# A hand-placed attention and SwiGLU kernel: the order of its last 621 statements is replaced by another one

## The chip, the cores and the metric

The kernel runs on one core of a Trainium2 chip. The metric is the device time of one execution in microseconds (us). Three runs of the kernel before gave 215.81, 215.92 and 216.0, so the median is 215.92. One more execution was recorded by the profiler; all durations here come from that one.

A core has five engines with an instruction queue each: TensorE (PE in the profile, with its weight loads listed as PEld), VectorE (DVE), ScalarE (ACT), GpSimd (POOL) and SyncE (SP), which only issues transfers. Each engine takes its instructions in the order in which the program gives them and waits at an instruction until its operands are there and its output may be written.

## The reference

Block-wise linear attention with a decay per head, over four batches of 768 tokens, eight heads of 64, feeds a SwiGLU feed-forward layer:

```python
for b in range(nb):                       # blocks of 64 tokens
    intra = np.einsum('bhic,bhjc->bhij', qb, kb) * Dmask[None]
    intra = np.einsum('bhij,bhjd->bhid', intra, vb)
    inter = np.einsum('bhid,bhde->bhie', qb * lam_pow[None], kv_state)
    out[:, :, sl] = intra + inter
    kv_state = lam_block * kv_state + np.einsum('bhsd,bhse->bhde', kb * rev_pow[None], vb)
x = out.transpose(0, 2, 1, 3).reshape(3072, 512)
g = x @ w_gate                            # 512 x 1536
return (g / (1 + np.exp(-g)) * (x @ w_val)) @ w_out      # 1536 x 512
```

## The kernel before, in words

**Groups and tiles.** The tokens are cut into twelve groups `g`. A group is one pair of 128-token blocks of one batch. Two groups make a tile `t` of 512 tokens, so there are six tiles, 0 to 5.

**Attention of a group.** `load_fp32` (L103) brings k, q and v from memory by SP. `kcast` (L277) and `qcast` (L281) cast, `v_scale` (L257) multiplies v by its decay (line L260), and `dma_transpose` (L265) has SP transpose q and k. The rest is on TensorE, in 64x64 tiles. `scores` multiplies q and k (L347 for groups up to 5, L383 for the later ones); `mask` (L356) multiplies the scores by the causal decay on DVE. `upd_mm` (L390, matmuls in L408) forms a group's part of the state, which `sadd`, `kvn`, `kvm` and `kv0c` accumulate on DVE, ACT and POOL. `inter` (L530, L541) applies the state to q, and `intra` (L547, L554) adds the masked scores times v to the same PSUM banks. Between the two stands `guard` (L523), an ACT copy of one column out of one of these banks (L525), so that `intra` starts only once `inter` is done. `evr` (L566) casts the sum into the tile's x.

**Feed-forward of a tile.** Tiles 0 to 3 use `ffn_gate` (L592, matmuls L600, SiLU on ACT L605) and `ffn_val` (L607, matmuls L618, product on DVE L622), one call for each 128 columns of d_ff. Tiles 4 and 5 use `uprod` (L731, L755) in the blocks that `unit` opens, a form with seven products in place of eight, whose combined operands come from `w_combo` and `x_combo`; `silu` and `mu` finish them. The output product of tile 0 is `ffn_out` (L629, L638). That of tiles 1 to 5 is `oprod` (L799, L814): `oprod(t, g, k)` is product k of group g, again seven of them, with sums of columns from `hsum`. After some k, ACT or DVE copies a quarter of the result into an output buffer (L817 to L829).

**Stores.** `store(t, g, r, c0, c1)` (L792, transfer L795) writes columns c0 to c1 of one 128-token block: 256 KB for 512 columns. SP issues it. The last product of the kernel, `oprod(5, 1, 3)`, brings its own stores: half of the result is copied by ACT and stored by ACT's queue, the other half copied by DVE and stored by SP, 64 KB each:

```python
        if k == 3 and last and g:
            for c, (fn, eng) in enumerate(((act, nc.scalar), (dve, nc.sync))):
                c0, c1 = c * HD // 2, (c + 1) * HD // 2
                fn(out=O[0][:, HD + c0:HD + c1], in_=Bb[:, c0:c1])
                store(t, g, 0, HD + c0, HD + c1, eng)
```

**The order.** From the end of the helper functions on, the kernel is a flat list of calls. The order of the list is the order on every engine: no scheduler moves anything (`tc.manual_schedule()`). A call that issues work on several engines puts it at this place in each of their queues. `use(6); ffn_gate(1, 8, 0, 2)` says into which of the eight PSUM banks the next call writes; `unit` and `out_new` name six banks for a group of products. A call that takes a bank waits until the bank's last reader, on ACT or DVE, has finished. The attention matmuls of a group are placed among the feed-forward matmuls of earlier tiles, so that masks and casts have time to run beside full matmuls. In the part that the change touches (L1035 to the end), the 64x64 matmuls come in 18 unbroken stretches, which this text calls visits.

Of the kernel before, what the change touches and what calls it, by code (L numbers as in the profile page):

```python
# [37 lines left out]
def _body(ctx, tc, nc, q, k, v, lam, moe_w_gate, moe_w_val, moe_w_out, out):  # L38
# [998 lines left out]
    mask(3, 1, 0)  # L1037
    mask(3, 0, 0)
    mask(3, 0, 1)
# [3 lines left out]
    use(7); ffn_val(1, 8, 0, 2)  # L1043
    mask(3, 1, 1)
    use(2); ffn_gate(1, 9, 0, 2)
    use(4); ffn_gate(1, 10, 0, 2)
    use(6); ffn_val(1, 9, 0, 2)
    use(0, 1); op_new(3)
    inter(3, True)
    use(2); ffn_val(1, 10, 0, 2)  # L1050
    guard(3)
    intra(3, False)
    use(3, 4); upd_mm(4)
    evr(3, 0, DVEC)
    kcast(5)
    evr(3, 1, ACTC)
    use(7); ffn_gate(1, 11, 0, 2)
    sadd(3, 1)
    sadd(4, 0)
    use(2); ffn_val(1, 11, 0, 2)  # L1060
    kvn(4, 0, ACTC)
    use(6); ffn_gate(1, 0, 2, 4)
    use(1); ffn_gate(1, 1, 2, 4)
    use(0); ffn_gate(1, 2, 2, 4)
    sadd(4, 1)
    qcast(5, nc.vector)
    use(5); ffn_gate(1, 3, 2, 4)
    use(2); ffn_val(1, 1, 2, 4)
    use(7); ffn_val(1, 2, 2, 4)
    use(6); ffn_val(1, 0, 2, 4)  # L1070
    use(1); ffn_gate(1, 4, 2, 4)
# [4 lines left out]
    use(3); ffn_gate(1, 5, 2, 4)  # L1076
    use(2, 0, 6, 4); scores(4)
    v_scale(5, nc.gpsimd)
    kvm(3, nc.gpsimd)
    wo_cast()  # L1080
    wo_cast()
    wo_cast()
    wo_cast()
    mask(4, 0, 1)
    mask(4, 1, 1)
    use(3); ffn_val(1, 3, 2, 4)
    mask(4, 1, 0)
    use(5); ffn_gate(1, 6, 2, 4)
    use(7); ffn_val(1, 4, 2, 4)
    use(4); ffn_gate(1, 7, 2, 4)  # L1090
    use(3); ffn_val(1, 5, 2, 4)
    use(1); ffn_gate(1, 8, 2, 4)
    use(7, 4); op_new(4)
    use(0); ffn_gate(1, 9, 2, 4)
    use(6); ffn_val(1, 9, 2, 4)
    mask(4, 0, 0)
    use(3); ffn_val(1, 6, 2, 4)
    inter(4, True)
    guard(4)
    w_combo(0, 0, (0, 3))  # L1100
    use(6); ffn_val(1, 7, 2, 4)
    intra(4, False)
    use(3, 5); upd_mm(5)
    evr(4, 1, ACTC)
    evr(4, 0, ACTC)
    new_xt(3)
    use(1); ffn_gate(1, 10, 2, 4)
    use(0); ffn_val(1, 8, 2, 4)
    use(4); ffn_gate(1, 11, 2, 4)
    use(7); ffn_gate(2, 0, 0, 2)  # L1110
    use(0); ffn_val(2, 0, 0, 2)
    wo_cast(ACTC)
    use(2); ffn_gate(2, 1, 0, 2)
    wo_combo(0)
    sadd(5, 0)
    use(1); ffn_val(1, 10, 2, 4)
    wo_cast()
    kvn(5, 0, ACTC)
    use(4); ffn_out(0, 0)
    use(0); ffn_val(1, 11, 2, 4)  # L1120
    use(7); ffn_gate(2, 2, 0, 2)
    use(4); ffn_gate(2, 3, 0, 2)
    use(1, 6); op_new(5)
    inter(5, True)
    use(3, 2, 7, 0); scores(5)
    kvm(4, nc.vector)
    mask(5, 1, 0)
    mask(5, 0, 0)
    mask(5, 0, 1)
    w_combo(1, 0, (0, 3))  # L1130
    sadd(5, 1)
    wo_combo(1)
    mask(5, 1, 1)
    guard(5)
    kcast(6)
    use(4); ffn_out(0, 1)
    qcast(6, nc.vector)
# [3 lines left out]
    load_fp32(7, nc.sync, v, "v")  # L1141
    hs_new(1)
    use(7); ffn_out(0, 2)
    intra(5, False)
    evr(5, 0, ACTC)
    evr(5, 1, ACTC)
    hs_new(1)
    use(2); ffn_out(0, 3)
    hsum(1, 0, 0, 6, 0, 1)
    hsum(1, 0, 0, 6, 1, 2)  # L1150
    hsum(1, 1, 0, 6, 1, 2)
    wo_combo(2)
    hsum(1, 2, 0, 6, 0, 1)
    use(7); ffn_gate(2, 0, 2, 4)
    use(5); ffn_val(2, 1, 0, 2)
    use(0); ffn_val(2, 3, 0, 2)
    use(6); ffn_val(2, 2, 0, 2)
    use(4); ffn_val(2, 0, 2, 4)
    hsum(1, 1, 0, 6, 0, 1)
    use(5); ffn_gate(2, 1, 2, 4)  # L1160
    hsum(1, 2, 0, 6, 1, 2)
    wo_combo(3)
    v_scale(6, nc.vector)
    use(7); ffn_gate(2, 2, 2, 4)
    use(2); ffn_gate(2, 3, 2, 4)
    use(3); ffn_val(2, 2, 2, 4)
    hsum(1, 3, 0, 6, 0, 1)
    use(7); ffn_val(2, 1, 2, 4)
    use(0); ffn_gate(2, 4, 0, 4)
    use(5); ffn_val(2, 4, 0, 4)  # L1170
    use(1); ffn_gate(2, 5, 0, 4)
    kcast(7)
    use(3, 4); scores(6)
    use(6, 2); upd_mm(6)
    mask(6, 0, 1)
    use(7); ffn_val(2, 5, 0, 4)
    sadd(6, 0)
    kvm(5, nc.gpsimd)
# [5 lines left out]
    out_new(1, (0,), [0, 1, 7], 0)  # L1184
    oprod(1, 0, 1)
    kvn(6, 0, ACTC)
    w_combo(0, 1, (0, 3))
    use(4); ffn_val(2, 3, 2, 4)
    sadd(6, 1)
    use(5); ffn_gate(2, 6, 0, 4)  # L1190
    oprod(1, 0, 7)
    oprod(1, 0, 2)
    kvn(6, 1, ACTC)
    v_scale(7, nc.vector)
    sadd(6, 2)
    mask(6, 0, 0)
    kv0c(3, ACTC)
    use(4); ffn_gate(2, 7, 0, 4)
    kvn(6, 2, ACTC)
    oprod(1, 0, 6)  # L1200
    sadd(6, 3)
    use(6); ffn_val(2, 6, 0, 4)
    hsum(1, 3, 0, 6, 1, 2)
    oprod(1, 0, 5)
    oprod(1, 0, 4)
    use(0); ffn_val(2, 7, 0, 4)
    oprod(1, 0, 3)
    store(1, 0, 1, 0, 512, None)
    store(1, 0, 0, 0, 512, None)
    use(3, 7); op_new(6)  # L1210
    inter(6, True)
    use(0, 4); upd_mm(7)
    use(2, 6); scores(7)
    kvm(6, nc.vector)
    sadd(7, 0)
    v_scale(8, nc.gpsimd, 0, 4)
    guard(6)
    kvn(7, 0, ACTC)
    mask(7, 0, 0)
    sadd(7, 1)  # L1220
    intra(6, False)
    evr(6, 1, ACTC)
    use(1); ffn_gate(2, 8, 0, 4)
    kvn(7, 1, ACTC)
    kcast(8)
    sadd(7, 2)
# [457 lines left out]
```

## Time and profile before

| what | value |
|---|---|
| median of three runs | 215.92 us (215.81 to 216.0) |
| the profiled execution's own time | 215.75 us |
| its span (first to last recorded event) | 214.0 us |
| TensorE busy | 207.5 us, 97% of the span, 2801 matmuls |
| DVE, ACT, POOL busy | 157.5, 131.8 and 50.9 us |
| granted TensorE clock | 1.00 |
| moved by DMA | 39.77 MB, 186 GB/s in the mean |
| stores by SP of L795, 256 KB each | median 2.7 us from issue to landing |

How to read it. The shares of busy time are means over the span. The slices divide the span into 40 equal parts and give the busy share of each in tenths. The chain that ended last is followed back from the last instruction, at each step to what released it. A row of the timeline gives the start, the busy time from the start of the first to the end of the last instruction in a run of equal ones, the engine, the line, the operation and the number of instructions; because matmuls are pipelined, the busy time of a row reaches past the start of the next row. In square brackets stands the idle time before and what ended it.

### The profile page before, as it was taken

To read this page: it belongs to the slowest core of one execution; us is meant where nothing else is said; L and a number is where in the kernel's file an instruction comes from. 1 tells how busy PE (TensorE), PEld (TensorE's weight loads), DVE (VectorE), ACT (ScalarE), POOL (GpSimd) and SP (SyncE) were. 2 spreads that over 40 slices of the span, in tenths; PEclk is the share of its full clock that TensorE was granted. 3 is DMA by queue.
4 is the path that set the end of the run, shared out by engine and by line. 5 is a ranking of instruction groups with operands and counts; after the bars stand their busy time and mean duration, and the time that the engine had idled before them with its cause. 6 is when DMAs were issued, how large, how long until landed. Compare 5 with 4: busy or idle time off the path is not lost.

```text
span 214.0 us, 6802 instructions
## 1 busy us (share of the span) xinstructions
PE 207.5 (97%) x2801; PEld 153.0 (72%) x2801; DVE 157.5 (74%) x302; ACT 131.8 (62%) x283; POOL 50.9 (24%) x72
## 2 busy tenths in 40 slices
PE   7799999999999999999999999999999999999993
PEld 3466455888886558767654545888888888888883
DVE  1673447679774798889779899999887589982851
ACT  6788576657446443667677385946873677536522
POOL 6585755704472010300101030040200000000200
PEclk9999999999999999999999999999999999999999
DMA  6999999999996697989677869776000500005014
GB/s 187 343 352 373 378 365 324 266 256 222 356 335 132 168 280 188 240 204 261 156 189 163 208 144 248 185 69 228 6 3 3 196 0 3 0 0 199 0 54 147
DMA packets 82177, 39.77 MB, mean 186 GB/s; under 512 B 45410, under 2 KB 77794, under 8 KB 82146
## 3 DMA queue, kind: packets, MB, share of 16 engines
q1 hardware_dynamic: 80946, 38.74, 66.7%
q10 hardware_dynamic: 1200, 0.59, 1.0%
q8 instruction: 22, 0.36, 0.7%
q14 instruction: 9, 0.07, 0.1%
HBM read 28.31 MB, written 6.29 MB: 162 GB/s over the span
## 4 chain that ended last, share of the span: by engine, by line
PE 92%; SPq 3%; DMA 2%; POOL 1%; issue 0%; ACT 0%; DVE 0%
PE bank L814 22%; PE bank L600 20%; PE bank L618 20%; PE bank L755 17%; PE bank L638 5%; SPq L109 2%; DMA v<-in_v_dram 2%; PE bank L541 2%; PE bank L554 2%; PE bank L408 1%; PE bank L347 1%; POOL v_s L260 1%; PE bank L383 1%; PE bank L310 0%; ACT kvf L501 0%
## 5 line engine op out<-in xcount | busy, mean ns | idle before, releaser
L622 DVE TENSOR_TENSOR h<-sil,bank 128x256 bf16<-128x256 bf16 (+1 forms) x67 | 35.0, 532 | 21.4 <-PE bank L618 17.2
L618 PE MATMUL bank<-xt,wv_sb 128*128 128x256 bf16 (+1 forms) x276 | 50.2, 314 | 0.0
L600 PE MATMUL bank<-xt,wg_sb 128*128 128x256 bf16 (+1 forms) x276 | 50.1, 315 | 0.0
L605 ACT ACTIVATE sil<-bank 128x256 bf16<-128x256 f32 (+1 forms) x67 | 31.6, 477 | 22.3 <-PE bank L600 15.7
L618 PEld LDWEIGHTS <-wv_sb 128*128 128x128 bf16 x276 | 26.6, 98 | 14.7
L600 PEld LDWEIGHTS <-wg_sb 128*128 128x128 bf16 x276 | 26.1, 98 | 12.9
L260 POOL TENSOR_TENSOR v_s<-v,dec 128x512 bf16<-128x512 f32 (+1 forms) x15 | 18.6, 1254 | 60.9 <-DMA v<-in_v_dram 19.8
L814 PEld LDWEIGHTS <-h 128*128 128x128 bf16 x240 | 23.5, 98 | 3.6
L814 PE MATMUL bank<-wo_sb,h 128*128 128x256 bf16 x180 | 22.3, 273 | 0.0
L814 PEld LDWEIGHTS <-hs 128*128 128x128 bf16 x180 | 17.5, 98 | 3.4 <-DVE hs L673 0.2
L362 DVE TENSOR_TENSOR ssb<-bank,causal 128x512 bf16<-128x512 f32 x24 | 15.5, 684 | 3.6 <-PE bank L347 3.5
L814 PE MATMUL bank<-wt,hs 128*128 128x256 bf16 x120 | 15.6, 272 | 0.0
L755 PEld LDWEIGHTS <-ws 128*128 128x128 bf16 x144 | 14.0, 98 | 1.8
L755 PE MATMUL bank<-xs,ws 128*128 128x256 bf16 x96 | 13.9, 272 | 0.0
L763 DVE TENSOR_TENSOR bank<-bank,es 128x512 f32<-128x512 f32 x12 | 8.3, 697 | 7.2 <-PE bank L755 4.4
L780 DVE TENSOR_TENSOR h<-sil,bank 128x512 bf16<-128x512 bf16 x18 | 11.8, 679 | 1.5 <-ACT sil L774 1.2
L780 POOL TENSOR_TENSOR h<-sil,es 128x512 bf16<-128x512 bf16 x1 | 1.2, 1162 | 46.7 <-DVE es L765 46.7
L774 ACT ACTIVATE sil<-bank 128x512 bf16<-128x512 f32 x18 | 10.2, 593 | 2.1 <-PE bank L755 2.1
L638 PE MATMUL bank<-wo_sb,h 128*128 128x512 bf16 x48 | 10.9, 379 | 0.0
L755 PE MATMUL bank<-xt,wv_sb 128*128 128x256 bf16 x72 | 10.8, 273 | 0.0
L443 ACT CAST kvn<-kvf 64x256 bf16<-64x256 f32 x22 | 8.9, 403 | 3.1 <-DVE kvf L489 2.7
L278 ACT CAST qk<-kraw 128x1024 bf16<-128x1024 f32 x9 | 9.4, 1042 | 1.8 <-DMA kraw<-in_k_dram 1.8
(127 smaller groups left out, 342.9 us busy)
## 6 DMA issues: line engine op xcount, KB each, us to landing
out_dram<-osb SPq DMA_DIRECT2D x22, 256.0 KB, 2.7
v<-in_v_dram SPq DMA_DIRECT2D x18, 256.0 KB, 4.3
woraw<-in_moe_w_out_dram SPq DMA_DIRECT2D x6, 512.0 KB, 9.1
kraw<-in_k_dram SPq DMA_DIRECT2D x24, 128.0 KB, 3.2
qraw<-in_q_dram SPq DMA_DIRECT2D x24, 128.0 KB, 3.8
wraw<-in_moe_w_gate_dram SPq DMA_DIRECT2D x5, 512.0 KB, 6.9
wraw<-in_moe_w_val_dram SPq DMA_DIRECT2D x5, 512.0 KB, 6.7
kraw<-in_k_dram SPq DMA_DIRECT2D x4, 512.0 KB, 6.3
```

Source lines behind the costliest of these rows:

```text
L260: eng.tensor_tensor(out=st[("vs", g)][:, h0:h1], in0=st[("v", g)][:, h0:h1].rearrange("p h (s d) -> p h s d", s=2), in1=vfac(g, h0, h1), o ...
L278: fn(out=qk_new(g)[:, 0].rearrange("p s (h d) -> p h s d", h=H), in_=st[("kraw", g)].rearrange("p h (s d) -> p h s d", s=2))
L362: nc.vector.tensor_tensor(out=st[("ssb", g)][:, h2, 2 * c:2 * c + 2].rearrange("p a s n -> p a (s n)"), in0=st[("sp", g, c, h2)].rearrange ...
L600: nc.tensor.matmul(gp[:, n0:n1], wg_sb[:, mc, fs], xt[:, g0:g1, mc].rearrange("p g b n -> p g (b n)"), start=(mc == 0 and n0 == 0), stop=( ...
L605: nc.scalar.activation(sil[:, 0:N], gp[:, 0:N], AF.Silu)
L618: nc.tensor.matmul(vp[:, n0:n1], wv_sb[:, mc, fs], xt[:, g0:g1, mc].rearrange("p g b n -> p g (b n)"), start=(mc == 0 and n0 == 0), stop=( ...
L622: nc.vector.tensor_tensor(out=h_sb[:, fc % FH, b0:b1].rearrange("p b n -> p (b n)"), in0=sil[:, 0:N], in1=vp[:, 0:N], op=ALU.mult)
L638: nc.tensor.matmul(ps, st[("h", t, fc // FH)][:, fc % FH, b], wo_sb[:, fc, c0:c1], start=(fc == 0), stop=(fc == FC - 1))
L755: nc.tensor.matmul(o[i][:, fi * 256:fi * 256 + 256], lhs(c, 2 * j + fi), rhs(c), start=(k < 2 and fi == 0 and c == 0), stop=(c == KH - 1), ...
L774: nc.scalar.activation(sil[half, r], unit_src(t, j, half, r)[0], AF.Silu)
L780: eng.tensor_tensor(out=st[("h", t, half)][:, 2 * j:2 * j + 2][:, :, r:B:2], in0=v3(st[("u", t, j)][4][half, r]), in1=v3(unit_src(t, j, ha ...
L814: nc.tensor.matmul(o, lhs(f), rhs(f), start=(k in (1, 7) and f == 0), stop=(f == FH - 1), skip_group_check=True)
```

## The change

The change replaces the list from L1035 to the end by another order of the same 621 statements. No statement is added or dropped. Banks are chosen anew. Two half pieces of `v_scale` and the two `kvm` of groups 3 and 4 trade places between DVE and POOL.

The visits of groups 3, 4, 10 and 11 are joined. A plus sign stands between parts of one visit:

| before | after |
|---|---|
| scores 3 + update 3, inter 3, intra 3 + update 4 | scores 3 + update 3, inter 3 + update 4 + intra 3 |
| scores 4, inter 4, intra 4 + update 5 | scores 4 + inter 4, intra 4 + update 5 |
| scores 11, inter 10 + update 11, intra 10 | scores 11 + inter 10, intra 10 + update 11 |
| the other nine | the same nine, in other surroundings |

That makes 15 visits in place of 18. The stores of tile 1 now stand between `dma_transpose(10)` and the loads of group 11, and one of them between the loads of q and v. Those of tile 4 stand behind the first products of tile 5. Among the last statements, three stores of tile 5 now stand behind `oprod(5, 1, 3)`, which issues stores of its own. The `...` lines mark what is left out of the diff.

```diff
     use(0, 1, 2, 3); scores(3)
     use(4, 5); upd_mm(3)
...
     use(7); ffn_val(1, 8, 0, 2)
+    use(4); ffn_gate(1, 9, 0, 2)
+    sadd(3, 1)
     mask(3, 1, 1)
-    use(2); ffn_gate(1, 9, 0, 2)
-    use(4); ffn_gate(1, 10, 0, 2)
-    use(6); ffn_val(1, 9, 0, 2)
-    use(0, 1); op_new(3)
+    use(2, 4); op_new(3)
+    use(1); ffn_gate(1, 10, 0, 2)
+    use(6); ffn_gate(1, 11, 0, 2)
+    use(7); ffn_val(1, 9, 0, 2)
     inter(3, True)
-    use(2); ffn_val(1, 10, 0, 2)
     guard(3)
+    use(1, 0); upd_mm(4)
     intra(3, False)
-    use(3, 4); upd_mm(4)
     evr(3, 0, DVEC)
...
+    use(2, 5); op_new(4)
+    use(0, 6, 3, 4); scores(4)
+    inter(4, True)
+    v_scale(5, nc.gpsimd)
+    kvm(4, nc.gpsimd)
...
     dma_transpose(10)
+    store(1, 0, 1, 0, 512, None)
+    store(1, 0, 0, 0, 512, None)
     store(1, 1, 1, 0, 512, None)
-    store(1, 1, 0, 0, 512, None)
     load_fp32(11, nc.sync, k, "kraw")
     load_fp32(11, nc.sync, q, "qraw")
+    store(1, 1, 0, 0, 512, None)
     load_fp32(11, nc.sync, v, "v")
...
+    dma_transpose(11)
+    store(2, 0, 1, 0, 512, None)
+    unit(4, 0, (5, 2, 1, 3, 6, 0))
+    uprod(4, 0, 0, 0)
+    uprod(4, 0, 0, 1)
+    oprod(2, 1, 5)
+    uprod(4, 0, 1, 1)
+    uprod(4, 0, 3, 0)
+    silu(4, 0, 0, 0)
+    uprod(4, 0, 1, 0)
+    uprod(4, 0, 2, 0)
+    uprod(4, 0, 2, 1)
+    use(5); ffn_val(3, 5, 0, 4)
+    uprod(4, 0, 3, 1)
...
-    use(5, 3); scores(11)
+    uprod(4, 0, 4, 0)
+    use(5, 7); op_new(10)
+    use(4, 2); scores(11)
+    inter(10, True)
     mask(11, 0, 0)
     mask(11, 0, 1)
-    uprod(4, 0, 3, 0)
-    uprod(4, 0, 2, 1)
-    silu(4, 0, 0, 0)
-    uprod(4, 0, 4, 0)
     uprod(4, 0, 5, 0)
...
+    guard(10)
+    intra(10, False)
+    use(2, 4); upd_mm(11)
...
-    inter(10, True)
-    use(7, 0); upd_mm(11)
...
-    intra(10, False)
...
     store(4, 0, 1, 0, 512, None)
     store(4, 1, 1, 0, 512, None)
+    oprod(5, 0, 2)
     store(4, 0, 0, 0, 512, None)
     store(4, 1, 0, 0, 512, None)
...
-    oprod(5, 0, 1)
-    oprod(5, 1, 1)
-    oprod(5, 0, 2)
+    oprod(5, 1, 7)
+    oprod(5, 1, 6)
+    oprod(5, 0, 7)
+    hsum(5, 3, 4, 6, 0, 2)
+    oprod(5, 0, 6)
+    oprod(5, 1, 5)
+    oprod(5, 1, 4)
+    oprod(5, 0, 5)
+    oprod(5, 1, 2)
     store(5, 0, 0, 0, 256, None)
-    oprod(5, 1, 2)
     store(5, 1, 0, 0, 256, None)
-    oprod(5, 0, 7)
-    oprod(5, 1, 7)
-    oprod(5, 0, 6)
-    oprod(5, 1, 6)
-    hsum(5, 3, 4, 6, 0, 2)
-    oprod(5, 0, 5)
-    oprod(5, 1, 5)
-    hsum(5, 3, 2, 4, 0, 2)
     oprod(5, 0, 4)
+    oprod(5, 0, 3)
+    oprod(5, 1, 3)
     store(5, 0, 1, 0, 512, None)
-    oprod(5, 1, 4)
     store(5, 1, 1, 0, 512, None)
-    oprod(5, 0, 3)
     store(5, 0, 0, 256, 512, None)
-    oprod(5, 1, 3)
```

828 lines of the change are left out of this document (405 added, 423 removed).

## The prediction

> **What bounds the kernel now.** I read the busy shares first (part 1 of the page), then the shares of the chain that ended last (part 4), then the busy time of each engine in single stretches, then single rows of the timeline.
>
> ```profile
> PE 207.5 (97%) x2801; PEld 153.0 (72%) x2801; DVE 157.5 (74%) x302; ACT 131.8 (62%) x283; POOL 50.9 (24%) x72
> ...
> PE 92%; SPq 3%; DMA 2%; POOL 1%; issue 0%; ACT 0%; DVE 0%
> 47.00:210.70 163.70, 163.70 (x2236) 125.17 (x2232) 131.79 (x246) 98.42 (x215) 22.97 (x21) 1.00 0.59 149
> 110.00:130.00 20.00, 20.00 (x212) 9.85 (x210) 17.94 (x30) 13.91 (x30) 3.10 (x3) 1.00 0.75 184
> 130.00:145.00 15.00, 15.00 (x233) 11.89 (x232) 14.13 (x27) 10.38 (x26) 2.53 (x2) 1.00 0.80 153
> ```
>
> TensorE is the bound. The reordered statements start at line 1035, which the trace reaches at about 47 us, and from there to 210.70 PE is busy all 163.70 us (third line of rows: stretch, its length, then busy time and count of PE, PEld, DVE, ACT and POOL, the granted clock, here 1.00, DMA share and GB/s). So in this part only three things can move the time: the matmul work itself with its switches, a wait that PE does not have today, and what comes after the last matmul. The last two lines name the engine that is nearest to causing such a wait: DVE is busy 90% and 94% of these stretches.
>
> **What a visit costs.** The change keeps every matmul and joins stretches of attention matmuls (64x64 tiles), called visits. Counted in the old and new text, from line 1035 on there are 18 before and 15 after. Rows of the timeline (start, busy us, engine, line) around the visit that holds `scores(11)` alone, and one row from inside a longer visit:
>
> ```profile
> 145.28 0.60 PE L755 MATMUL bank<-xt,wv_sb 128*128 128x256 bf16 x4
> 145.81 0.45 PE L383 MATMUL bank<-qkt 64*64 64x64 bf16 x32
> 146.19 0.61 PE L755 MATMUL bank<-xt,wg_sb 128*128 128x256 bf16 x4
> ...
> 147.51 0.60 PE L755 MATMUL bank<-xs,wg_sb 128*128 128x256 bf16 x4
> 147.95 0.60 PE L755 MATMUL bank<-xt,wv_sb 128*128 128x256 bf16 x4
> 121.67 0.44 PE L383 MATMUL bank<-qkt 64*64 64x64 bf16 x32
> 121.93 0.26 PE L408 MATMUL bank<-v_s,qk 64*64 64x64 bf16 x7
> ```
>
> Four full matmuls between full ones go from 147.51 to 147.95, 0.44 us. Those ahead of the visit need 145.28 to 145.81, 0.53: entry 0.09. The 32 small matmuls need 0.26 inside a visit (121.67 to 121.93) and 0.38 when full ones follow (145.81 to 146.19): exit 0.12. A visit therefore costs 0.21 us, and three fewer give 3 x 0.21 = -0.63. Ends: nothing (the price returns inside the joined visits) to -0.9 (the early visits have other matmuls around them, 128x512 and `ffn_out`, and I let them be half as dear again).
>
> The Trainium skill (TensorE: Matmul & The Clock Gate, "Step-by-step: what each phase is for") says that the drain of one matmul overlaps the fill of the next; applied to a switch, that would make a visit free and the sum below 0.63 higher. The row shows 0.09 and 0.12 where it would have none, so here the trace disagrees, and I go by the row; what the rule would make of the time is rival C below.
>
> **The joined visit of group 3.** `guard` is an ACT copy of one column that makes `intra` wait until `inter` has finished in the same banks. Before, four full matmuls stand between them:
>
> ```profile
> 50.02 0.41 PE L541 MATMUL bank<-qkt,kvn 64*64 64x128 bf16 x8
> 50.36 0.61 PE L618 MATMUL bank<-xt,wv_sb 128*128 128x256 bf16 x4
> 50.47 0.16 ACT L525 COPY guard<-bank 128x1 f32<-128x1 f32 x1 [0.34 <-PE bank L541]
> 50.90 0.64 PE L554 MATMUL bank<-ssb,v_s 64*64 64x128 bf16 x32
> ```
>
> The guard ends at 50.47 + 0.16 = 50.63, 0.61 after `inter` starts. After, only `upd_mm(4)` stands between: `inter` 0.34 - 0.12 = 0.22 and 32 update matmuls 0.26, together 0.48. PE waits 0.13, and with the 0.04 that lies between the end of `inter` (50.43) and the guard (50.47) as the way back, 0.17. Ends: 0 (intra's first head free earlier) to 0.5, if ACT is just in a 0.38 SiLU when `inter` ends. Everything behind on PE shifts by this; ACT's and DVE's work shifts with it and gains slack. For groups 4, 10 and 11 full matmuls still separate `inter` from `intra`, so their guards cost nothing.
>
> **The new order of the rest.** Same statements, so the same busy time on each engine; the work of a few `v_scale` and `kvm` pieces only trades places between DVE and POOL. Full matmuls move at no price as long as their banks and operands are there. Walking the new text engine by engine with the rows' durations, the operands arrive 0.1 to 0.9 us ahead of PE. The thinnest: `scores(10)` wants the transposed q and k of `dma_transpose(10)` at about 130.7 and, with the landing of 3.8 us that this transpose has now, gets them at about 130. On SP, the three stores of tile 1 now behind `dma_transpose(10)` (two before) put the loads of group 11 one issue, 0.4 us, later; the last piece of `k` is issued at about 132 and lands 3.0 later, and `kcast(11)`, its first user, runs at 136 today and stands later in the new text; POOL's `v_scale(11)` runs at 139. `store(1,1,0)` between the `q` and `v` loads has its data long since. The output buffers it frees are wanted again by tile 2's copies, some 5 us later. `ffn_val(3,5)` comes late, but its gate's SiLU is done and the columns it feeds are used only by the tile-3 products. Sum of new waits: +0.1. Low end -0.1 (PE has nothing to lose but gaps that the 163.70 does not show), high end +1.5, worked out with the second rival.
>
> **The tail.** Here the text of the change moves work onto the path that ends the span. SP executes its queue in order. Before, `oprod(5,1,3)`, the last product, came after all other stores, and its own 64 KB store by SP was the last thing in the queue:
>
> ```profile
> 211.16 0.29 DVE L833 COPY osb<-bank 128x128 f32<-128x128 f32 x1 [2.16 <-ACT osb L833]
> 211.48 0.33 SPq L795 DMA_DIRECT2D out_dram<-osb  x1
> out_dram<-osb SPq DMA_DIRECT2D x2, 256.0 KB, 2.1
> out_dram<-osb SPq DMA_DIRECT2D x1, 128.0 KB, 1.7
> out_dram<-osb SPq DMA_DIRECT2D x1, 64.0 KB, 1.6
> 166.99 1.82 SPq L795 DMA_DIRECT2D out_dram<-osb  x4
> 168.30:170.30 2.00, 2.00 (x20) 1.80 (x19) 0.37 (x1) 1.78 (x4) 0.00 (x0) 1.00 1.06 407
> ```
>
> The three lines in the middle are the landing times of the tail's stores. After, `store(5,0,1)`, `store(5,1,1)` (256 KB each) and `store(5,0,0)`'s second half (128 KB) stand behind that 64 KB store, which waits for the last DVE copy at 211.45. Before, the last three of these went out between 209.30 and 210.94; now they cannot start before 211.8. Issues back to back: four took 1.82 in the row from 166.99, the first alone 0.33 with a gap, so three more take 1.4. The bytes give the same: 640 KB at the 407 GB/s that four such stores reach (last line) are 655,360 B / 407 GB/s = 1.61. The last store issues at 211.48 + 1.4 = 212.9 and lands 1.7 later, 214.6, where the last landing was 211.48 + 1.6 = 213.1: +1.5. With the bytes a little behind the issues I take +1.6. Ends: +1.1 (three issues of 0.33, landing 0.1 longer) and +2.5 (1.4 and the landing of a 256 KB store in a crowd, 2.7, which is the page's median for such stores, in place of 1.6). If the last matmul shifts, all of this shifts with it: nothing covers it.
>
> The stores of tile 4 also move later in the text, behind the first products of tile 5; with 14 products of 0.655 us (six matmuls of 0.109) behind them, SP is free of them 6 us before the end: 0.
>
> **Sum**, on the profiled execution's own 215.75: -0.63 + 0.17 + 0.1 + 1.6 = +1.24, so 217.0; that execution lies 0.17 below the median of the three runs, 215.92, so the forecast is 217.2.
>
> **The rivals.**
> A, faster: the tail costs nothing. It would be so if the SP queue did not hold the three stores behind the one that waits, so that they went out under the last products as now. For it: their data is ready 0.8 us or more before the last copy ends. Against it: in the trace of before, SP's issues come in the order of the text, each after the one before. Then -0.63 + 0.17 + 0.1 = -0.36: 215.6. It decides from a tail under 0.36. Chance 0.10.
> B, a new wait in the dense middle: DVE at 94% gets behind PE, or the transposes of group 10 land late. For it: the slowest of the nine transposes landed after 5.7 us instead of 3.8, 1.9 more against 0.7 of margin, so +1.2; `scores(10)` stops PE, and its masks come later on the engine that is fullest. To this comes DVE's lag, up to 0.3 (half a mask), so 1.5 in all. Against it: DVE still has 0.87 us free in its fullest 15, and this transpose runs beside the same loads today. Then 217.2 + 1.2 to 1.5: about 218.5. Chance 0.20.
> C, the visits give nothing back because the switch cost shows up inside: 217.2 + 0.63 = 217.8. Chance 0.08. For it: nothing in the rows but their model of a matmul's end. Against it: L383 takes 0.26 inside a visit, with no switch cost ahead of L408.
> The main line has 0.62, its own range 216.7 to 218.1 (tail +1.1 to +2.5 with the rest unchanged).
>
> **Range and chances.** About 0.2% (0.43 us) is what a measurement of this kernel can tell from no change. Of A, 0.06 is faster than 215.5 and 0.04 lies within; of the main line 0.03 lies within (small tail, no new waits). So faster 0.06, same 0.07, slower 0.87. The range 216.1 to 218.7 leaves out A and the upper part of B.
>
> **What would show it.** Steps: from 121 us on the same L755 and L814 groups as before, and 15 visits with entries of 0.09; in the new order PE busy without a gap except one of about 0.2 ahead of L554 near 51 us; the last PE matmul at about 210.3 instead of 210.7; in SP's queue four L795 issues back to back at the end, the last some 1.4 us after the first, and a span end 5.0 us after the last matmul instead of 214.04 - 210.66 = 3.4. The prediction is wrong if the last matmul ends later than 210.9 (then a new wait, to be found by PE's waits), or if the end comes within 4 us of it (then rival A).

## The result, and the profile after

The changed kernel takes 219.28 us in the median (218.76 to 220.58, six runs), the kernel before 216.03 in the six runs beside them. The ratio is 1.016, with a 95% interval of 1.0129 to 1.019. The forecast was 217.2 and its range ended at 218.7: the direction was right, the size was not, 3.25 us in place of 1.2.

The profiled execution of the changed kernel took 218.92 us, 3.17 more than that of the kernel before. From the page after: the busy times, the shares of the chain, and a stretch (length, then busy time of PE, PEld, DVE, ACT, POOL).

```profile
PE 207.5 (96%) x2796; PEld 153.5 (71%) x2801; DVE 157.9 (73%) x302; ACT 131.5 (61%) x283; POOL 51.0 (23%) x72
...
PE 80%; DMA 5%; DVE 4%; ACT 4%; SPq 2%; issue 2%; ACTq 0%; DVEq 0%
...
47.00:211.90 164.90, 163.75 (x2232) 125.43 (x2236) 132.15 (x246) 98.13 (x215) 23.13 (x21) 1.00 0.58 147
```

PE's busy time has not changed, but its share of the chain fell from 92% to 80%; DVE, ACT and transfers have come into it. Where PE was busy all 163.70 us of its stretch, it now has 1.15 us without work. Short gaps do not show there, because the modelled end of a matmul reaches past the start of the next; a few of the tenths are matmuls missing from the records (2796 of 2801). The clock is 1.00 in both.

The end of the kernel, by the timeline after:

```profile
212.01 0.27 ACT L833 COPY osb<-bank 128x128 f32<-128x128 f32 x1 [0.28 <-PE bank L814]
212.31 0.29 DVE L833 COPY osb<-bank 128x128 f32<-128x128 f32 x1 [2.49 <-ACT osb L833]
212.63 0.33 SPq L795 DMA_DIRECT2D out_dram<-osb  x1
213.06 0.41 SPq L795 DMA_DIRECT2D out_dram<-osb  x1
213.52 0.42 SPq L795 DMA_DIRECT2D out_dram<-osb  x1
214.04 0.40 SPq L795 DMA_DIRECT2D out_dram<-osb  x1
```

The four stores go out one behind the other, the last 1.41 us after the first. So the 3.17 us divide as follows.

| piece | before | after | difference |
|---|---|---|---|
| end of the last DVE copy | 211.45 | 212.60 | +1.15 |
| from there to the end of the span | 2.6 | 4.5 | +1.9 |
| outside the span | 1.71 | 1.83 | +0.1 |

The first line is the matmul work. Three visits fewer took about 0.6 off it, so the new gaps come to some 1.8 us more than the kernel before has, whose own short gaps add up to 0.4. The PE rows below, from the timeline after, show the longest of them and four more. (An expected start is the start before, plus 0.109 for each matmul.)

```profile
137.09 0.82 PE L814 MATMUL bank<-wt,hs 128*128 128x256 bf16 x6 [0.72 <-ACT bank L817]
...
151.23 1.05 PE L755 MATMUL bank<-xt,ws 128*128 128x256 bf16 x8
152.27 0.60 PE L755 MATMUL bank<-xt,wg_sb 128*128 128x256 bf16 x4
...
154.51 0.60 PE L755 MATMUL bank<-xt,wg_sb 128*128 128x256 bf16 x4
155.07 0.60 PE L755 MATMUL bank<-xt,wv_sb 128*128 128x256 bf16 x4
...
177.06 0.60 PE L755 MATMUL bank<-xt,wg_sb 128*128 128x256 bf16 x4
177.62 0.60 PE L755 MATMUL bank<-xs,ws 128*128 128x256 bf16 x4
...
181.11 0.60 PE L755 MATMUL bank<-xt,wv_sb 128*128 128x256 bf16 x4
181.68 0.60 PE L755 MATMUL bank<-xs,ws 128*128 128x256 bf16 x4
```

At 137.09 PE stands 0.88 us start to start beyond the pitch (0.72 between modelled ends). In the uprods, 152.27 comes 0.17 late, 155.07 0.12, 177.62 0.12 and 181.68 0.13. Each of these four waits for an instruction on another engine and starts 0.05 us after its end: the first behind DVE's L489, the other three behind copies of ACT (L759). To these come 0.28 among the gates at 113.8 and 0.19 behind the guard of group 3, where the last of the 28 update matmuls starts at 50.97:

```profile
50.69 0.46 PE L408 MATMUL bank<-v_s,qk 64*64 64x64 bf16 x28
50.95 0.16 ACT L525 COPY guard<-bank 128x1 f32<-128x1 f32 x1 [0.34 <-PE bank L541]
51.16 0.64 PE L554 MATMUL bank<-ssb,v_s 64*64 64x128 bf16 x32
```

### The profile page after: what moved, and what is told of

Its sections match the earlier page's. It is cut to its first block, busy times and chain, and to the rows that moved or that the text cites. A ratio compares the mean times of both kernels' runs of the same rounds, so it can differ in the third digit from the quotient of the medians.

```text
span 217.1 us, 6782 instructions
## 1 busy us (share of the span) xinstructions
PE 207.5 (96%) x2796; PEld 153.5 (71%) x2801; DVE 157.9 (73%) x302; ACT 131.5 (61%) x283; POOL 51.0 (23%) x72
## 4 chain that ended last, share of the span: by engine, by line
PE 80%; DMA 5%; DVE 4%; ACT 4%; SPq 2%; issue 2%; ACTq 0%; DVEq 0%
PE bank L814 18%; PE bank L755 17%; PE bank L618 17%; PE bank L600 16%; PE bank L638 5%; DMA kraw<-in_k_dram 4%; PE bank L554 2%; PE bank L541 2%; DMA v<-in_v_dram 1%; PE bank L408 1%; PE bank L347 1%; DVE ssb L362 1%; ACT qk L278 1%; SPq L109 1%; SPq L124 1%
## 5 line engine op out<-in xcount | busy, mean ns | idle before, releaser
L618 PEld LDWEIGHTS <-wv_sb 128*128 128x128 bf16 x276 | 26.7, 98 | 14.2
L814 PE MATMUL bank<-wo_sb,h 128*128 128x256 bf16 x180 | 22.9, 273 | 0.0
L638 PE MATMUL bank<-wo_sb,h 128*128 128x512 bf16 x44 | 10.3, 379 | 0.3 <-issue 0.2
L755 PEld LDWEIGHTS <-wv_sb 128*128 128x128 bf16 x96 | 9.4, 98 | 1.5
```

The source lines that it names most:

```text
L618: nc.tensor.matmul(vp[:, n0:n1], wv_sb[:, mc, fs], xt[:, g0:g1, mc].rearrange("p g b n -> p g (b n)"), start=(mc == 0 and n0 == 0), stop=( ...
L638: nc.tensor.matmul(ps, st[("h", t, fc // FH)][:, fc % FH, b], wo_sb[:, fc, c0:c1], start=(fc == 0), stop=(fc == FC - 1))
L755: nc.tensor.matmul(o[i][:, fi * 256:fi * 256 + 256], lhs(c, 2 * j + fi), rhs(c), start=(k < 2 and fi == 0 and c == 0), stop=(c == KH - 1), ...
L814: nc.tensor.matmul(o, lhs(f), rhs(f), start=(k in (1, 7) and f == 0), stop=(f == FH - 1), skip_group_check=True)
```

## The experiments

All times are medians in us. The ratio is to the kernel before, whose median was between 215.86 and 216.06 beside each of them; it is worked out from all runs, not from the two medians, and can differ from their quotient by some tenths of a per cent. The kernel before was no steadier in its range: beside these experiments its runs spread over 1.1 to 2.8 us (215.56 to 218.31 beside tail_back). A difference of a few tenths between two medians says little by itself.

| kernel | median (range) | ratio, 95% interval |
|---|---|---|
| tail_back | 217.84 (216.96 to 219.58) | 1.0069 (1.0041 to 1.0098) |
| before_tail | 217.72 (217.44 to 218.9) | 1.0071 (1.0045 to 1.0098) |
| tail_thin | 218.81 (218.47 to 219.51) | 1.0109 (1.0059 to 1.016) |
| act_late | 218.72 (218.13 to 219.85) | 1.011 (1.0073 to 1.0147) |
| tail_and_act | 217.28 (216.51 to 217.53) | 1.0047 (1.0032 to 1.0063) |
| join_3 | 216.5 (216.16 to 217.49) | 1.0011 (0.9989 to 1.0034) |
| split4 | 220.14 (220.03 to 220.49) | 1.0191 (1.0171 to 1.0211) |
| last_tile | 215.88 (215.53 to 216.65) | 0.9996 (0.9983 to 1.0009) |
| one_copy | 216.12 (215.83 to 216.64) | 0.999 (0.9966 to 1.0014) |
| all_mended | 217.43 (216.7 to 217.75) | 1.0056 (1.0035 to 1.0076) |
| qcast_late | 217.09 (216.1 to 218.13) | 1.0042 (1.0017 to 1.0068) |
| all_two | 217.43 (216.04 to 219.05) | 1.0051 (1.0026 to 1.0076) |
| early_only | 216.73 (216.12 to 217.83) | 1.0038 (1.0021 to 1.0056) |
| late_only | 218.47 (218.43 to 219.38) | 1.0119 (1.0099 to 1.014) |
| late_mended | 216.84 (216.56 to 217.45) | 1.0044 (1.0028 to 1.006) |
| early_six | 216.69 (216.1 to 217.43) | 1.0028 (1.0012 to 1.0044) |
| all_three | 216.3 (215.62 to 217.06) | 1.002 (1.0007 to 1.0033) |

### The tail

tail_back, in the changed kernel:

```diff
     store(5, 1, 0, 0, 256, None)
+    store(5, 1, 1, 0, 512, None)
     oprod(5, 0, 4)
+    store(5, 0, 1, 0, 512, None)
     oprod(5, 0, 3)
+    store(5, 0, 0, 256, 512, None)
     oprod(5, 1, 3)
-    store(5, 0, 1, 0, 512, None)
-    store(5, 1, 1, 0, 512, None)
-    store(5, 0, 0, 256, 512, None)
```

> The changed kernel with one thing put back: the three stores of tile 5 stand ahead of oprod(5,1,3) again. Theory (the tail costs 1.9 us, because three stores wait behind the store that needs the last copy): the last DVE copy stays at about 212.6 in the span, the span ends 2.6 us after it instead of 4.5, and the time falls by 1.9 to about 217.4. Rival (the end is set by the bytes that are still to be written, not by their place in SP's queue): the same bytes have to go out, so the gain is under 0.5 and the time stays near 218.9.

Its median is 1.4 us below that of the changed kernel; the ratio fell from 1.016 to 1.0069, by 0.9% or 2.0 us. In its profile the last copy ends at 213.29 and the span at 216.1, 2.8 after it instead of 4.5. The tail itself gave 1.7. The copy was expected at 212.6 and came 0.7 later, because PE has a gap of 0.73 at 106.7 that is not in the profile of the changed kernel; it is taken up in the last group. The median stayed 0.4 above the expected 217.4, in runs that spread over 2.6 us.

before_tail, in the kernel before:

```diff
     oprod(5, 0, 4)
-    store(5, 0, 1, 0, 512, None)
     oprod(5, 1, 4)
-    store(5, 1, 1, 0, 512, None)
     oprod(5, 0, 3)
-    store(5, 0, 0, 256, 512, None)
     oprod(5, 1, 3)
+    store(5, 0, 1, 0, 512, None)
+    store(5, 1, 1, 0, 512, None)
+    store(5, 0, 0, 256, 512, None)
```

> The kernel before with one thing changed: the three stores of tile 5 stand behind oprod(5,1,3), all else as it was. Theory: +1.9, so about 217.9, with the last matmul where it was. If the tail's cost needs the rest of the new order (other products just before the end, tile 4's stores later): under +1, so below 217.

It took 217.72, 1.7 more than the kernel before. From its timeline:

```profile
211.88 0.29 DVE L833 COPY osb<-bank 128x128 f32<-128x128 f32 x1 [2.16 <-ACT osb L833]
212.20 1.81 SPq L795 DMA_DIRECT2D out_dram<-osb  x4
```

The span ended at 216.7, 4.5 after the copy's end at 212.17: the whole tail of the changed kernel, with nothing else of the change. The order of these three statements is its cause. The copy itself ended 0.72 later than in the profile of the kernel before, by a gap of 0.65 at 53 us, where nothing was edited: this order, too, has gaps in some executions and not in others.

tail_thin is the changed kernel with fewer columns in the three stores:

```diff
-    store(5, 0, 1, 0, 512, None)
-    store(5, 1, 1, 0, 512, None)
-    store(5, 0, 0, 256, 512, None)
+    store(5, 0, 1, 0, 128, None)
+    store(5, 1, 1, 0, 128, None)
+    store(5, 0, 0, 256, 320, None)
```

> The changed kernel, its last three stores cut to a quarter of their columns (160 KB instead of 640 KB; the rest of these blocks of the output is not written). If the tail is the three issues on SP: the last issue stays 1.4 us behind the first and the time falls only by what the last store lands sooner, 0.3 to 0.6. If it is the bytes (640 KB at 407 GB/s are 1.6 us): the time falls by 1.2 to 1.6.

The median fell by 0.5 us. In the profile the last copy ended at 212.73 and the span at 216.6, 3.9 after it: a quarter of the bytes brought back 0.6 of 1.9 us. The last issue still comes 1.40 behind the first. So of the 1.9 some 1.4 are the issues on SP, and 0.5 is the landing of a larger store in a crowd (2.07 from issue to landing for the last 128 KB, where the kernel before's last 64 KB needed 1.59).

### The gap behind ACT

In the changed kernel ACT makes the three kvn casts of group 10 ahead of the copies that `oprod(2, 0, 6)` accumulates on. act_late:

```diff
     sadd(10, 1)
-    kvn(10, 1, ACTC)
...
-    kvn(10, 2, ACTC)
     oprod(2, 0, 7)
     oprod(2, 0, 1)
     oprod(2, 1, 1)
+    kvn(10, 1, ACTC)
+    kvn(10, 2, ACTC)
     kv0c(7, ACTC)
```

> The changed kernel with kvn(10,1) and kvn(10,2) moved behind oprod(2,1,1) on ACT's queue, so that the copies which oprod(2,0,6) waits for (line 817) come 1.2 us earlier. Theory (the 0.88 us gap of TensorE at 137.1 is ACT's backlog): the gap goes and the time falls by 0.8 to 0.9, to about 218.4. Rival (the next operand is as late, or the gap returns further on): under 0.3.

Timeline of the changed kernel, then of act_late, ACT and PE around the place:

```profile
134.44 0.82 ACT L443 CAST kvn<-kvf 64x256 bf16<-64x256 f32 x2
135.26 0.41 ACT L445 CAST kvn<-kvf 128x256 bf16<-128x256 f32 x1
135.68 0.82 ACT L443 CAST kvn<-kvf 64x256 bf16<-64x256 f32 x2
136.41 0.36 ACT L819 COPY osb<-bank 128x256 f32<-128x256 f32 x1
136.67 0.63 ACT L817 COPY bank<-bank 128x256 f32<-128x256 f32 x2
```

```profile
133.57 2.78 PE L814 MATMUL bank<-wo_sb,h 128*128 128x256 bf16 x24
134.40 0.82 ACT L443 CAST kvn<-kvf 64x256 bf16<-64x256 f32 x2
135.39 0.74 ACT L817 COPY bank<-bank 128x256 f32<-128x256 f32 x2
136.19 0.82 PE L814 MATMUL bank<-wt,hs 128*128 128x256 bf16 x6
```

The copies start at 135.39 instead of 136.67, and the next product at 136.19 instead of 137.09, right behind the 24 matmuls. PE's gap is gone, and the last matmul is 0.88 earlier. The profiled execution took 218.13, 0.79 less. The medians differ by 0.56 and the ratios by 0.5%, 1.1 us, but their intervals overlap: what the edit removes is shown by the profile, its worth in the median only roughly.

tail_and_act joins the two edits.

> The changed kernel with both put right: the three stores ahead of oprod(5,1,3), and kvn(10,1) and kvn(10,2) behind oprod(2,1,1). Theory (two costs that have nothing to do with each other, 1.9 and 0.9): they add up, and about 216.4 remains, 0.4 above the kernel before: 0.6 less by three visits, 1.0 more by the waits left. Rival (each hides part of the other, or a new wait takes the place): above 217.2.

It came to 217.28, not 216.4: the rival's side of the bound, 2.0 below the changed kernel where 2.8 was expected. In the profiled execution (217.0) the two mended places were clean, but PE had a gap of 0.63 at 106.7 that the profile of the changed kernel had not shown. It is taken up in the last group.

### What a visit is worth

join_3 takes the join of group 3 alone into the kernel before:

```diff
     inter(3, True)
-    use(2); ffn_val(1, 10, 0, 2)
     guard(3)
-    intra(3, False)
     use(3, 4); upd_mm(4)
+    intra(3, False)
+    use(2); ffn_val(1, 10, 0, 2)
```

> The kernel before with one thing of the change: ffn_val(1,10) no longer stands between inter(3) and intra(3), upd_mm(4) takes its place, so that the three make one visit. Theory: 0.2 less for the visit, 0.2 more for the wait behind the guard, together nothing: TensorE's last matmul within 0.1 of where it was and the time the same within 0.2%. Rival (the guard is hidden by upd_mm(4)): 0.2 faster. Rival (the visit saves nothing): 0.2 slower.

Its timeline around that visit, PE and the guard:

```profile
50.58 0.41 PE L541 MATMUL bank<-qkt,kvn 64*64 64x128 bf16 x8
51.00 0.45 PE L408 MATMUL bank<-v_s,qk 64*64 64x64 bf16 x32
51.03 0.16 ACT L525 COPY guard<-bank 128x1 f32<-128x1 f32 x1 [0.34 <-PE bank L541]
51.27 0.62 PE L554 MATMUL bank<-ssb,v_s 64*64 64x128 bf16 x32
51.82 0.28 PE L618 MATMUL bank<-xt,wv_sb 128*128 128x256 bf16 x1
```

From the start of `inter` to the next full matmul: 51.82 - 50.58 = 1.24, and 0.44 for `ffn_val(1, 10)`, which now comes behind it, make 1.68. In the kernel before the same work took from 50.02 to 51.75, 1.73. The join moved PE by -0.05: what the visit gave, the wait behind the guard took, as expected. The time is the same within its interval. The last matmul, expected within 0.1 of its old place, is 1.2 later in this profile. Of that, 0.56 lies ahead of the visit; the rest are gaps at 53 us (0.31 and 0.21) and at 147 us (0.13). Whether those at 53 us come from the edit is open, so the run speaks for the visit alone.

split4 cuts four visits of the kernel before in two by moving one statement from ahead of the visit to between its parts, for instance:

```diff
-    oprod(1, 1, 5)
     hs_new(2)
     use(7, 3); op_new(7)
     inter(7, True)
     use(6, 2); upd_mm(8)
+    oprod(1, 1, 5)
     use(0, 5); scores(8)
```

> The kernel before with four of its visits cut in two: one product or ffn_val that stood ahead of the visit is put between its parts (oprod(1,0,3) with its stores, oprod(1,1,5), ffn_val(3,3), ffn_val(3,10)). Theory (a visit costs 0.20 for its entry and exit): TensorE's last matmul comes 4 x 0.20 = 0.8 later, and the time rises by 0.8 to about 216.8. Rival (the drain of one matmul overlaps the fill of the next, a visit is free): no change of the last matmul, under 0.2.

It rose by 4.2 us, far over either number. PE's waits in it (engine, line, waited for: us in total, times, longest):

```profile
PE bank L541 <- ACT sil L605: 0.7, 1, 0.7
...
PE bank L408 <- DVE h L622: 0.5, 1, 0.5
PE bank L383 <- DMA qkt<-qk: 0.5, 1, 0.5
...
PE bank L541 <- ACT kvn L443: 0.2, 1, 0.2
```

Each cut brought the first part of a visit forward by the 0.65 or 0.86 us of the statement that no longer stood ahead of it, and most of these parts then waited for their operands. As a price of a visit its time is inconclusive; it shows how little room these visits have ahead of them. Start to start, with the larger waits taken off, the four visits that were cut are 0.10 to 0.22 us longer than in the kernel before, which fits a price of about 0.2 without fixing it. The price rests on rows like those of the prediction, on join_3, and on the joined visits of the changed kernel itself. Measured from the last full matmul ahead to the first one behind, these are shorter than their parts before by 0.24 (group 3, the wait behind the guard taken off), 0.22 (group 4) and 0.18 us (groups 10 and 11): 0.63 in all. The Trainium skill (TensorEngine Tiling (Array Packing), "Key Properties") says that a change of the tiling mode drains TensorE. The rows agree, with 0.09 on the way in and 0.12 on the way out.

### The last copies

last_tile gives DVE's half of the last product a buffer of its own:

```diff
-                fn(out=O[0][:, HD + c0:HD + c1], in_=Bb[:, c0:c1])
+                src = O[0]
+                if c:
+                    src = kv_pool.tile([128, 2 * HP * D], FP32, name="es", tag="ups", bufs=4)
+                fn(out=src[:, HD + c0:HD + c1], in_=Bb[:, c0:c1])
+                st[("o", t, g)][3][0] = src
```

> The kernel before, with a buffer of its own for the half of the last product that DVE copies, so that this copy needs nothing of ACT's. Theory (DVE waits for ACT's copy because both write one buffer): the two copies start together, the span ends 0.25 to 0.3 earlier, and the time falls to about 215.7. Rival (they wait for one another at the PSUM bank that both read): no change.

one_copy lets ACT copy all 256 columns and has both queues store a half:

```diff
-            for c, (fn, eng) in enumerate(((act, nc.scalar), (dve, nc.sync))):
-                c0, c1 = c * HD // 2, (c + 1) * HD // 2
-                fn(out=O[0][:, HD + c0:HD + c1], in_=Bb[:, c0:c1])
-                store(t, g, 0, HD + c0, HD + c1, eng)
+            act(out=O[0][:, HD:DM], in_=Bb)
+            store(t, g, 0, HD, HD + HD // 2, nc.scalar)
+            store(t, g, 0, HD + HD // 2, DM, nc.sync)
```

> The kernel before, with the last product copied by ACT alone (256 columns, 0.37 us as in the rows of line 829) and then stored in two halves by the queues of ACT and SP. Theory (ACT's and DVE's copies of one PSUM bank run one after the other, 0.59 us from first start to last end): the last store is issued 0.2 us earlier and the span ends 0.2 earlier, about 215.7. Rival (the landing sets the end, whichever issue comes first): no change.

Neither moved the time. In last_tile the DVE copy still starts at 212.07, with the end of ACT's copy (211.78 + 0.27): not the buffer holds it, so presumably the bank that both read. In one_copy the copy takes 0.37 instead of 0.59 from first start to last end, but the span ends 3.2 after the copy's start in both kernels. The two stores, now issued together, land after 1.65 and 1.81 us, where those of the kernel before landed after 1.59 and 1.66: the landing sets the end.

### Which half the rest is in

Up to the visit that ends with intra(9), the old and the new order hold the same statements but for two, which the expectations name at the seam. early_only is the new order up to there and the old one behind it; late_only is the reverse. Every statement is there, but these two and late_mended compute part of the output wrongly, presumably because some PSUM banks are taken over at the seam with another history than their order was made for. They serve to place the cost and nothing else.

> The order of the change up to the visit that ends with intra(9), and from out_new(2) on the order of before (ffn_val(3,5) stands at the seam). It holds two of the three joined visits (groups 3 and 4) and the change's order of the loads and casts, but neither the line-817 gap nor the uprods of the change nor its tail. Theory (this half has fixed gaps of 0.2 at the guard of group 3 and 0.2 to 0.3 at 113.8, against 0.4 for two visits, and a varying wait of 0 to 1.7 behind late loads): 216.0 to 217.2, a little slower and more scattered than before. Rival (the loads' varying waits are of no account and all the cost lies in the second half): 215.8, not slower.

> The order of before up to that place and the order of the change from out_new(2) on (x_combo(4,0) stands at the seam): one joined visit, the uprods of the change, and its tail. Theory: +1.9 for the tail, +0.4 for the gaps in the uprods (0.67 less the 0.28 that the order of before has there), -0.2 for the visit, and 0 to 0.9 for the copies of line 817, which stand behind less on ACT here: 218.1 to 219.0. Rival (most of the cost is in the first half): below 217.7, the tail alone.

> late_only with the three stores ahead of oprod(5,1,3) and kvn(10,2) behind oprod(2,1,1). Theory: the tail and the gap of line 817 are gone, +0.4 for the uprods and -0.2 for the visit remain: 216.1 to 216.4, the same as before within 0.2%, and with the narrow scatter of the kernel before. Rival (the second half has costs of its own that the profiles have not shown): above 216.8.

early_only costs 0.87 us, in runs that spread over 1.7 (1.3 for the kernel before beside them); late_only costs 2.61, and five of its six runs lie within 0.11 us. Together they make 3.5, against 3.25 for the whole change. That the sums agree is partly luck: the gap of 0.88 behind L817 is only 0.07 in late_only's profile, and its tail is 4.8 in place of 4.5. late_mended came to 216.84, 0.98 above the kernel before, 0.4 above what was expected. Its profile shows why: the last copy is 0.39 later than before (the uprods' gaps less a visit, and 0.24 at the seam), as expected, but the span ends 3.1 after the copy, not 2.6. The stores had been put ahead of the last product, yet five of them go out within 2.5 us there, since `oprod(5, 1, 2)` stands fourth from the end in the new order.

### What scatters in the first half

Timelines around 104 us of the changed kernel, whose profile has no gap there, and of tail_and_act, whose profile has one:

```profile
102.03 1.23 DVE L282 TENSOR_TENSOR qk<-qraw,qdn 128x1024 bf16<-128x1024 f32 x1 [1.84 <-DMA qraw<-in_q_dram]
...
103.50 0.95 DVE L680 TENSOR_TENSOR ws<-ws,wv_sb 128x1536 bf16<-128x1536 bf16 x1
103.68 2.69 POOL L260 TENSOR_TENSOR v_s<-v,dec 128x512 bf16<-128x512 f32 x2 [13.11 <-PE bank L600]
...
104.97 0.43 DVE L823 TENSOR_TENSOR bank<-bank,osb 128x256 f32<-128x256 f32 x1
105.80 0.82 PE L814 MATMUL bank<-wt,h 128*128 128x256 bf16 x6
```

```profile
102.38 1.23 DVE L282 TENSOR_TENSOR qk<-qraw,qdn 128x1024 bf16<-128x1024 f32 x1 [1.95 <-DMA qraw<-in_q_dram]
...
103.82 2.77 POOL L260 TENSOR_TENSOR v_s<-v,dec 128x512 bf16<-128x512 f32 x2 [13.48 <-DMA v<-in_v_dram]
103.86 1.82 DVE L680 TENSOR_TENSOR ws<-ws,wv_sb 128x1536 bf16<-128x1536 bf16 x1
...
106.20 0.42 DVE L823 TENSOR_TENSOR bank<-bank,osb 128x256 f32<-128x256 f32 x1
106.67 0.81 PE L814 MATMUL bank<-wt,h 128*128 128x256 bf16 x6 [0.47 <-DVE bank L823]
```

DVE stands 1.8 to 2 us before `qcast(8)` (L282) and waits for q, which it does not do at this place in the profile of the kernel before. After that `w_combo(1, 1)` (L680) takes 0.95 where it starts ahead of POOL's `v_scale`, and 1.82 where POOL started 0.04 earlier. The sum of L823 is then 1.2 later, and the product behind it waits. Seven of the profiles have the change's order of these queues (the changed kernel, tail_back, tail_thin, act_late, tail_and_act, all_mended and early_only). Four of them have the gap, 0.4 to 1.7 us long, and they are the four in which `w_combo(1, 1)` took 1.8. DVE waits for q in six of the seven, so the late q alone does not make the gap.

qcast_late, in tail_and_act:

```diff
-    qcast(8, nc.vector)
     kvm(6, nc.vector)
     w_combo(1, 1, (0, 3))
+    qcast(8, nc.vector)
```

> tail_and_act, with kvm(6) and w_combo(1,1), whose operands are there, ahead of qcast(8) on DVE's queue. Theory (the gap of TensorE at 106.7, 0.63 us in tail_and_act and 1.67 in all_mended, comes from DVE: it stands 1.95 us before qcast(8) and waits for q, and is late for the sum of line 823 afterwards): DVE's wait falls by 1.28 to about 0.7, the gap at 106.7 goes, and the time falls by 0.6 to 0.8 to about 216.6. Rival (q itself is late, so that dma_transpose(8) and then scores(8) wait in its place): the gap moves to 107 to 108 and the time stays within 0.3 of tail_and_act.

DVE's wait fell to 0.84 and the gap at 106.7 went, but the time did not follow: 217.09, 0.2 below tail_and_act, in runs that spread over 2.0 us. Its profiled execution (218.08) has gaps of 0.6 behind a late `v_scale` at 51.9 and of 0.9 behind a late transpose at 57.7, both of group 4 and far ahead of the edit. So the run does not tell what the edit gave; only the part of the theory about DVE's queue held.

all_mended and all_two add one repair to tail_and_act and to qcast_late, the one with last_tile's edit beside it, the other with one_copy's:

```diff
-    use(0); ffn_gate(3, 7, 0, 4)
     v_scale(9, nc.vector, 0, 4)
     use(7); ffn_val(3, 0, 0, 4)
+    use(0); ffn_gate(3, 7, 0, 4)
```

> tail_and_act, with a buffer of its own for DVE's last copy (-0.25 to -0.3) and with ffn_val(3,0) ahead of ffn_gate(3,7), so that the gate finds its bank read (the gap of 0.28 at 113.8 goes). Theory: about 215.9, the level of the kernel before, not under it by more than 0.2, since the wait behind the guard of group 3 (0.2) and those in the uprods at 152 to 158 and 177 to 182 (0.6) remain. Rival (margins so thin everywhere that the gaps return): above 216.6.

> qcast_late, with ffn_val(3,0) ahead of ffn_gate(3,7) (the gap at 113.8) and the last product copied by ACT alone. Theory: 0.2 and 0.2 to 0.3 less than qcast_late, about 216.1, the level of the kernel before within 0.2%: what three visits give is taken by the waits that remain at the guard of group 3 and in the uprods. Rival: above 216.6, because the order has no room for a late transfer.

Both landed at 217.43, on the rivals' side. The gap at 113.8 was gone in all_mended, but in its profiled execution q came so late that DVE waited 3.0 us, and PE's gap at 107.7 was 1.67. The profiled execution of all_two, its slowest at 219.05, has gaps of 0.95 at 51.6 and of 0.96 and 0.85 between 120 and 123 us. The small repairs gained nothing that can be measured here.

early_six therefore moves the chain, in tail_and_act. In the new order `dma_transpose(6)` stands some way behind the evictions of group 5; the transposes and loads of the next groups follow it on SP's queue.

```diff
     mask(5, 1, 1)
+    kcast(6)
+    qcast(6, nc.vector)
     w_combo(1, 0, (0, 3))
     hsum(1, 0, 0, 6, 1, 2)
     guard(5)
     use(5); ffn_out(0, 1)
+    dma_transpose(6)
+    load_fp32(7, nc.sync, k, "kraw")
+    load_fp32(7, nc.sync, q, "qraw")
+    load_fp32(7, nc.sync, v, "v")
...
-    kcast(6)
     evr(5, 1, ACTC)
-    qcast(6, nc.vector)
...
-    dma_transpose(6)
-    load_fp32(7, nc.sync, k, "kraw")
-    load_fp32(7, nc.sync, q, "qraw")
-    load_fp32(7, nc.sync, v, "v")
```

> tail_and_act, with kcast(6) and qcast(6) ahead of w_combo(1,0) and guard(5), and with dma_transpose(6) and the loads of group 7 right behind ffn_out(0,1): SP's chain from there (transpose 6, loads of 7, transpose 7, loads of 8) starts up to 2 us earlier. Theory (the first half is slower and scatters because this chain runs 0.5 to 1.6 us later in the order of the change than before, so that DVE stands waiting for q of group 8): DVE's wait for q at qcast(8) falls under 0.5, the gap at 106.7 goes, and the time falls from 217.3 to about 216.6, with a narrower scatter. Rival (a late load is not what costs; the thin places are spread over the whole half): no change within 0.3.

The transposes of groups 6, 7 and 8 in SP's queue, of the changed kernel and of early_six:

```profile
77.80 1.65 SPq L268 DMA_TRANSPOSE qkt<-qk  x1
...
90.59 2.55 SPq L268 DMA_TRANSPOSE qkt<-qk  x1
...
103.39 1.60 SPq L268 DMA_TRANSPOSE qkt<-qk  x1
```

```profile
76.28 1.78 SPq L268 DMA_TRANSPOSE qkt<-qk  x1
...
88.61 2.14 SPq L268 DMA_TRANSPOSE qkt<-qk  x1
...
102.31 1.61 SPq L268 DMA_TRANSPOSE qkt<-qk  x1
```

The chain is 1.1 to 2.0 us earlier, DVE no longer waits at `qcast(8)`, and the gap at 106.7 is gone. The median is 216.69, 0.6 below tail_and_act and 0.1 from the number expected; ten of eleven runs lie between 216.1 and 216.9. The intervals of the two ratios still overlap, and one profile without the gap is no proof: act_late, whose chain was not moved, has the same transposes at 78.03, 89.93 and 102.30, no wait at `qcast(8)` and no gap either. That the earlier chain brought the 0.6 us is likely, and not shown.

all_three adds the gate's repair to early_six and spreads the last stores:

```diff
     oprod(5, 0, 6)
+    oprod(5, 1, 2)
+    store(5, 0, 0, 0, 256, None)
+    store(5, 1, 0, 0, 256, None)
     oprod(5, 1, 5)
     oprod(5, 1, 4)
+    store(5, 1, 1, 0, 512, None)
     oprod(5, 0, 5)
-    oprod(5, 1, 2)
-    store(5, 0, 0, 0, 256, None)
-    store(5, 1, 0, 0, 256, None)
-    store(5, 1, 1, 0, 512, None)
     oprod(5, 0, 4)
```

> early_six, with ffn_val(3,0) ahead of ffn_gate(3,7) (the gap at 113.8), and with oprod(5,1,2) three products earlier, so that fewer stores stand close together at the end (the tail of the mended kernels is 2.8 us behind the last copy where the kernel before has 2.6). Theory: 0.2 and 0.2 less than early_six, 216.0 to 216.3, level with the kernel before. Rival: above 216.8.

216.3, as expected; its profile ends 2.6 after the last copy, like the kernel before. At a ratio of 1.002 (1.0007 to 1.0033) it is level with the kernel before or a little slower, and not faster. Its profiled execution was the fastest of the twelve (215.62), and there the last matmul is 0.12 earlier than in the profile of the kernel before: the 0.63 of three visits is a little more than the guard and the uprods take. What adds 0.4 in the median is in no profile.

## Why the prediction was wrong

- **What a visit costs: right.** The trace after has 15 visits, fourteen with the entry of 0.09 that the forecast used, and the joined ones are 0.63 shorter than their parts. Rival C fell.
- **The guard of group 3: right.** 0.17 was forecast; 0.19 was found in the changed kernel, and in join_3 it cancels the visit to within 0.05.
- **The tail: right in kind, too small.** 1.6 was forecast, 1.9 measured, and before_tail shows it alone. The issues take 1.4 as worked out. The mis-sized term is the landing: 1.7 was taken from a 128 KB store with few others beside it, and behind two of 256 KB it needs 2.1. Rival A fell.
- **The new order of the rest: this step failed.** "Sum of new waits: +0.1" should have read about +1.6 beside the 0.19 at the guard, with 0.88 at one place; the last matmul ended at 211.98, where anything past 210.9 was named as the sign of a new wait. The walk compared the arrival of operands with PE's need for each matmul, at the margins of 0.1 to 0.9 us. It did not follow ACT's queue ahead of `oprod(2, 0, 6)`, where three casts of 0.4 and 0.8 stand before a copy that PE needs (act_late). It also treated a load that arrives later as harmless while the matmul that uses it is far off. But `qcast(8)` is in DVE's queue, and DVE waits there for q with everything that stands behind. In the profiled execution of the changed kernel that wait cost PE nothing; in four others it stands ahead of a gap of 0.4 to 1.7. That the change moves each `dma_transpose` and so the loads behind it was said for groups 10 and 11 only.
- **Rival B** named a wait in the dense middle. Its 218.5 came nearest to the result, but by luck: `scores(10)` did not wait in the profile after, no single gap was 1.2 long, and the sum came from other places. A price for such waits should have been part of the main line, because the order of every queue was changed and PE had nothing to lose but time.
- One count was off and cost nothing: the stores of tile 4 have eleven products behind the last of them, not fourteen. SP issued that one at 202.16, long before the end.
- The rest of the difference between 218.92, the profiled execution, and 219.28 is scatter: the forecast gave one number for a kernel whose six runs spread over 1.8 us. The three runs of the kernel before that it started from spread over 0.2, and later ones over up to 2.8, so its 0.2% for what a measurement can tell was too small.

Not settled: the gaps of 0.5 to 0.6 us in all that remain in the uprods between 151 and 182 us were seen in every profile with the new second half, and were not tried by themselves. Their causes, like that of the 0.28 at 113.8, are read from the traces alone.

## What to carry to other kernels

In a kernel whose bounding engine has almost no gaps, a new order has little to win and every queue to lose in: look first for the stores that a last store now blocks, then walk ACT's, DVE's and SP's queues, not only PE's. A cast that waits for a load stops all that stands behind it on its engine: here waits of 1.95 and 3.0 us on DVE stood ahead of gaps of 0.63 and 1.67 in PE, although the matmul that needs the load comes 5 us after the cast. And where a kernel's runs scatter, a single profile does not show all of its gaps, nor does its absence there show that an edit removed a gap.

## What the runs showed of the hardware that was not expected

One DVE instruction of the same form, L680 with 128x1536 elements from two SBUF operands, the `w_combo(1, 1)` of the last group above, took 0.94 to 0.95 us in fourteen of the profiles and 1.80 to 1.83 in five. In the five a `v_scale` had started on POOL 0.03 to 0.54 us before and was still running. The Trainium skill (SBUF — State Buffer, "SBUF: two separate sides") says that DVE, with two SBUF inputs, and a GpSimd instruction that reads SBUF take a shared pair of ports in turn, for a whole instruction each. The rows agree: 0.95 and about 0.9 of waiting. In tail_and_act both starts follow a landing, DVE's that of q and POOL's that of v. Between it and the changed kernel the two starts moved by 0.2 us against each other, and that became 0.9.

The DMA transposes of groups 6 to 11 held SP's queue for 1.6 to 3.8 us (`dma_transpose(7)`: 1.67 in act_late, 2.55 in the changed kernel, 3.82 in all_mended), and the loads behind them came that much later.
